# k's halves swapped by GpSimd, the crossbar from the second batch on, and regrouped remainder work in a fused attention and MLP kernel

## The chip, the cores and the metric

The kernel runs on one core of one Trainium2 chip. The metric is the device time of one execution in microseconds (us); less is better. A core has TensorE (PE; its weight loads are PEld), VectorE (DVE), ScalarE (ACT), GpSimd (POOL) and SyncE (SP), which here only issues DMAs. "Crossbar" means the transpose done by a DMA (DMA_TRANSPOSE).

## The reference

Thresholded attention over 8 batches of 8 heads with 576 positions and head size 64, then a two-layer MLP over the 4608 tokens (512 to 2048 to 512).

```python
scores = scale * np.matmul(q, k.transpose(0, 1, 3, 2))
thresh = np.max(scores, axis=-1, keepdims=True) - tau
scores = np.where(scores >= thresh, scores, -1000000000.0)
scores = scores - np.max(scores, axis=-1, keepdims=True)
attn = np.exp(scores)
attn = attn / (np.sum(attn, axis=-1, keepdims=True) + 1e-09)
return np.matmul(attn, v).astype(np.float32)
...
x = np.ascontiguousarray(attn_out.transpose(0, 2, 1, 3)).reshape(B * S, H * D)
...
h = x @ w_in
g = h - np.tanh(h)
return (g @ w_out).astype(np.float32)
```

## The kernel before

Two heads make a pair; there are 32 pairs, four per batch. A head's 576 positions are 512 in four blocks of 128 and a remainder of 64. A pair has nine score tiles of 128 query rows by 576 keys: tiles 0 to 3 are the first head's blocks, tile 4 (kind "M") the remainders of both heads, 64 rows each, tiles 5 to 8 the second head's blocks. Of these, "A" and "B" tiles follow each other in twos.

q and k are split into a high and a low fp16 part (khl, qhl; from the second pair on GpSimd does it, L160 to L164), turned on TensorE (ps_k, ps_q, L186) and copied to SBUF by VectorE (kT, qT, L192). The scores are q times kT plus q times kS, where kS is kT with its two halves of 64 partitions swapped. Pair 0 gets kS from TensorE (L198), all others by two DMAs from SyncE (L208, L209).

The main loop runs one step per tile, and its order is written out by hand. Step s issues: nb of tile s+6 (L257), the scores of tile s+7 on TensorE (psS, L232 and L242) with VectorE's copy and row maximum (sc, L248), the masking activation of tile s+5 on ScalarE (z, L274), the exponentials of tile s (pT, L302 or L310), a share of the MLP (psH L391, tanh th L404, g L410, psY L417, yo L426), and the product with v of tile s-2 (psO, L341, for M tiles L329). Between z and pT the masked scores are turned. Tiles below NPE (72, the first two batches) are turned on TensorE into psZ (L293), the others through the crossbar (zT, L282). After a head's tiles follows the division by the row sums (rc, osb, L355 and L356), and after a pair emit_x turns its result for the MLP (psX, L367; the remainder L374; copies L381 and L382).

A table (PREP) says how many steps ahead of a pair's first scores its loads (16 to 14 steps), splits (8, 7), turns (5, 3) and the cast of v (4) are issued. The weights are loaded in 16 pieces and cast by GpSimd (L473), one piece every four steps up to step 56. Each batch's MLP layers run spread over the next batches' tiles; a last "batch" of all remainders (xR, 512 tokens) and what is left runs behind the loop. Its output goes out by one store per 128 tokens, from yo, which has two buffers (L433); scratch for scores (ps_big) has two buffers too.

Of the kernel before, what the change touches and what calls it, by code (L numbers as in the profile page):

```python
# [18 lines left out]
def kernel(  # L19
# [11 lines left out]
    nc = tc.nc  # L31
    P = 128

    B, H, S, D = q.shape
# [6 lines left out]
    QKSC = 256.0  # L41
# [4 lines left out]
    HPAIR = H // 2  # L46
# [3 lines left out]
    TPP = 9  # L50
    NTILE = NPAIR * TPP


    NPE = 2 * HPAIR * TPP
    W = 2 * S

    AHEAD = 7
# [6 lines left out]
    MB = 512  # L64
# [52 lines left out]
    ps_y = pool("ps_y", 1, space=PSUM)  # L117

    ctx.enter_context(tc.manual_schedule())
    warm = const.tile([P, 1], F32, name="warm")  # L120
    nc.vector.memset(warm, 0.0)
    nc.scalar.activation(out=warm, in_=warm, func=ACT.Exp)


    raws = {}
# [3 lines left out]
    def load(p, t):  # L129
        b, h0 = p // HPAIR, 2 * (p % HPAIR)  # L130
        hs = slice(h0, h0 + 2)
        src = {"k": k, "q": q, "v": v}[t]
        eng = nc.scalar if p == 0 and t == "q" else nc.sync
        r = raws[p, t] = raw_pool.tile([P, 10, D], F32, name=f"{t}raw", tag=t)
        n = 8 if t == "v" else 10
        eng.dma_start(
            out=r[:, 0:n, :].rearrange("p (h c) d -> p h (c d)", h=2)[:, :, 0 : 4 * D],
            in_=src[b, hs, 0:512, :].rearrange("h (p c) d -> p h (c d)", c=4),
        )
        if t == "v":  # L140
            rem = src[b, hs, 512:S, :].rearrange("h s d -> s h d")
# [7 lines left out]
    def split(p, t, fast=False):  # L149
        r = raws.pop((p, t))[:, 0:9, :]  # L150
        hl = hl_pool.tile([P, TPP, 2, D], FP16, name=f"{t}hl", tag=t)
        if fast:
            nc.scalar.mul(out=hl[:, :, 0, :], in_=r, mul=QKSC)
            nc.vector.scalar_tensor_tensor(
                out=hl[:, :, 1, :], in0=r, scalar=QKSC, in1=hl[:, :, 0, :],
                op0=ALU.mult, op1=ALU.subtract,
            )
        else:
            x = hl_pool.tile([P, TPP, D], F32, name="xs", tag="xs")
            nc.gpsimd.tensor_scalar(  # L160
                out=x, in0=r, scalar1=QKSC, scalar2=1.0, op0=ALU.mult, op1=ALU.mult
            )
            nc.gpsimd.tensor_copy(out=hl[:, :, 0, :], in_=x)
            nc.gpsimd.tensor_tensor(  # L164
                out=hl[:, :, 1, :], in0=x, in1=hl[:, :, 0, :], op=ALU.subtract
            )
        hls[p, t] = hl

    def split_v(p):
        r, vb = raws.pop((p, "v")), vbs[p % NV]  # L170
# [8 lines left out]

    mats = {}  # L180

    def turn(p, t):
        hl = hls.pop((p, t))
        ps = ps_big.tile([P, W], FP16, name=f"ps_{t}", tag="big")
        for c in range(TPP):
            nc.tensor.matmul(  # L186
                out=ps[:, c * P : (c + 1) * P],
                lhsT=hl[:, c, :, :].rearrange("p a d -> p (a d)"),
                rhs=ident_f16, is_transpose=True, start=True, stop=True,
            )  # L190
        m = qk_pool.tile([P, W], FP16, name=f"{t}T", tag=t)
        nc.vector.tensor_copy(out=m, in_=ps)  # L192
        mats[p, t] = m
        if t == "k" and p == 0:
            ps = ps_big.tile([P, W], FP16, name="ps_ks", tag="big")
            for c in range(TPP):
                for a in range(2):
                    nc.tensor.matmul(  # L198
                        out=ps[64 * a : 64 * a + 64, c * P : (c + 1) * P],
                        lhsT=hl[:, c, 1 - a, :],  # L200
                        rhs=ident_f16, is_transpose=True, start=True, stop=True,
                    )
            sw = qk_pool.tile([P, W], FP16, name="kS", tag="ks")
            nc.vector.tensor_copy(out=sw, in_=ps)
            mats[p, "ks"] = sw
        elif t == "k":
            sw = qk_pool.tile([P, W], FP16, name="kS", tag="ks")
            nc.sync.dma_start(out=sw[0:D, :], in_=m[D:P, :])  # L208
            nc.sync.dma_start(out=sw[D:P, :], in_=m[0:D, :])  # L209
            mats[p, "ks"] = sw  # L210


    MAIN = (slice(0, 512), slice(640, W))
# [101 lines left out]
    def attend(i):  # L315

        p, j = divmod(i, TPP)
        kd, vb = kind(j), vbs[p % NV]
        if kd == "A":
            return  # L320
        if j in (1, 6):
            ops[p, int(j > 4)] = ps_o.tile([P, 5, D + 1], F32, name="psO", tag="o")
        po = ops[p, int(j > 4)]
        if kd == "M":
            pt = pts.pop(i)
            for c in range(5):
                n = 64 if c == 4 else P
                for hh in range(2):
                    nc.tensor.matmul(  # L329
                        out=po[64 * hh : 64 * hh + 64, 4, :],  # L330
                        lhsT=pt[0:n, c * P + 64 * hh : c * P + 64 * hh + 64],
                        rhs=vb[0:n, hh, c, :], start=(c == 0), stop=(c == 4),
                    )
            return
        pt, hh = pts.pop(i), int(j > 4)

        for ab in range(2):
            blocks = [(4 * ab + ab + c, c) for c in range(4)]
            blocks.append((4, 4 + ab))
            for n, (blk, c) in enumerate(blocks):  # L340
                nc.tensor.matmul(  # L341
                    out=po[:, (j - 1 - 5 * hh) + ab, :],
                    lhsT=pt[:, blk * P : (blk + 1) * P], rhs=vb[:, hh, c, :],
                    start=(n == 0), stop=(n == 4),
                )
# [3 lines left out]
    def norm(p, hh):  # L349
        po = ops.pop((p, hh))  # L350
        if hh == 0:
            osb[p] = o_pool.tile([P, 5, 2, D], BF16, name="osb")
        n = 5 - hh
        rc = st_pool.tile([P, 5], F32, name="rc", tag="rc")
        nc.vector.reciprocal(out=rc[:, 0:n], in_=po[:, 0:n, D])  # L355
        nc.vector.tensor_tensor(  # L356
            out=osb[p][:, 0:n, hh, :], in0=po[:, 0:n, 0:D],
            in1=rc[:, 0:n].unsqueeze(2).to_broadcast([P, n, D]), op=ALU.mult,
        )

    xs = {}

    def emit_x(p):
        o = osb.pop(p)
        ps = ps_h.tile([P, S], BF16, name="psX", tag="h")
        for t in range(4):
            nc.tensor.matmul(  # L367
                out=ps[:, t * P : (t + 1) * P],
                lhsT=o[:, t, :, :].rearrange("p a d -> p (a d)"),
                rhs=ident_bf, is_transpose=True, start=True, stop=True,  # L370
            )
        for hh in range(2):
            s = slice(64 * hh, 64 * hh + 64)
            nc.tensor.matmul(  # L374
                out=ps[s, 512:576], lhsT=o[s, 4, 0, :], rhs=ident_bf[s, s],
                is_transpose=True, start=True, stop=True,
            )
# [4 lines left out]
        nc.vector.tensor_copy(out=xR[:, p % HPAIR, b, :], in_=ps[:, 512:S])  # L382


    gs, stores = {}, []
# [29 lines left out]
    def project(m, ms, part, ps, last):  # L415
# [5 lines left out]
        if part == 3:  # L421
            yo = y_pool.tile([P, d_model], F32, name="yo")
            if last:
                nc.scalar.copy(out=yo, in_=ps)
            else:
                nc.vector.tensor_copy(out=yo, in_=ps)  # L426
            if m < B:
                rows = out[m * S : m * S + MB, :].rearrange("(p c) n -> c p n", c=4)
                to = rows[ms]
# [3 lines left out]
            stores.append(lambda: nc.sync.dma_start(out=to, in_=yo))  # L433

    def layers(m, tail):

# [69 lines left out]
    for t in ("k", "q", "v"):  # L506
        load(0, t)
    for t in ("k", "q"):
        split(0, t, fast=True)
    for t in ("k", "q"):  # L510
        turn(0, t)
    split_v(0)
    for t in ("k", "q", "v"):
        load(1, t)
# [8 lines left out]
    for s in range(-AHEAD, NTILE + LAG + 3):  # L523
# [7 lines left out]
            shift(s + AHEAD - 1)  # L531
        if 0 <= s + AHEAD < NTILE:
            scores(s + AHEAD)
        if 0 <= s + MASK < NTILE:
            kink(s + MASK)
        bend()
# [79 lines left out]
```

## Time and profile before

| What | us |
|---|---|
| median of 3 runs (range) | 579.23 (577.52 to 580.37) |
| the profiled execution, its own time | 578.05 |
| its span | 576.3 |
| PE busy | 535.3 |
| DVE busy | 442.6 |
| ACT busy | 440.1 |
| POOL busy | 215.6 |

The span is what the profiler saw of the program; its time is a little longer. Busy time says how long an engine had work in flight, not whether the run waited for it; that is read from the chain of work that ended last, which goes back from the last instruction, at each step to what released it.

### The profile page before, as it was taken

What the parts mean: (1) busy time and instruction counts of PE and PEld (TensorE: products, weight loads), DVE (VectorE), ACT (ScalarE), POOL (GpSimd) and SP (SyncE); (2) the same over time, 40 slices, a digit from 0 to 9 for tenths busy, and PEclk for the clock granted to TensorE, in tenths of its full rate; (3) what the DMA queues carried; (4) which work ended last, traced back from release to release, by engine and by line L of the source; (5) the groups of instructions that cost most, each with busy time, mean ns of one, the idle gap of its engine ahead of it and who ended that gap; (6) DMA issues with size and microseconds to landing.
All of it is one profiled execution on the core that took longest, in us unless ns stands there. A gap on an engine that the chain in (4) does not pass through costs nothing.

```text
span 576.3 us, 13882 instructions
## 1 busy us (share of the span) xinstructions
PE 535.3 (93%) x5146; PEld 303.6 (53%) x5146; DVE 442.6 (77%) x1312; ACT 440.1 (76%) x634; POOL 215.6 (37%) x310
## 2 busy tenths in 40 slices
PE   3889899999999999998999999999999999999990
PEld 2566566665555555554555555555555555444440
DVE  3888888888988988888888888888889896444410
ACT  1889898898888898887898988888889888333400
POOL 6646683753433344444444343345333400000000
PEclk9999999999999999999999999999999999999996
DMA  6556755448889999779989999998999865110111
GB/s 180 170 170 175 211 171 160 138 109 176 176 180 183 180 197 197 173 179 185 174 192 182 186 196 178 188 203 189 179 185 176 184 128 120 38 38 36 38 45 46
DMA packets 186923, 89.48 MB, mean 155 GB/s; under 512 B 150632, under 2 KB 175208, under 8 KB 186856
## 3 DMA queue, kind: packets, MB, share of 16 engines
q1 hardware_dynamic: 186454, 88.31, 70.2%
q8 instruction: 40, 0.66, 0.5%
q10 hardware_dynamic: 402, 0.29, 0.2%
q14 instruction: 27, 0.22, 0.1%
HBM read 37.75 MB, written 9.44 MB: 82 GB/s over the span
## 4 chain that ended last, share of the span: by engine, by line
PE 75%; DMA 6%; ACT 6%; DVE 6%; POOL 2%; issue 1%; SPq 1%; ACTq 0%; POOLq 0%; DVEq 0%
PE psY L417 20%; PE psH L391 17%; PE psS L242 17%; PE psO L341 5%; PE ps_k L186 3%; PE psS L232 3%; ACT pT L302 3%; DVE sc L248 3%; DMA kS<-kT 2%; PE psHt L391 2%; PE psZ L293 2%; ACT z L274 2%; PE psO L329 2%; PE ps_q L186 2%; DMA out_dram<-yo 2%
## 5 line engine op out<-in xcount | busy, mean ns | idle before, releaser
L248 DVE TENSOR_SCALAR_CACHE_REDUCE sc<-psS 128x576 f32<-128x576 f32 x288 | 216.4, 751 | 24.4 <-PE psS L232 10.8
L274 ACT ACTIVATE z<-sc,nb 128x576 bf16<-128x576 f32 x256 | 195.5, 768 | 27.2 <-DVE nb L257 26.0
L417 PE MATMUL psY<-w_out_sb,g 128*128 128x512 bf16 x576 | 145.4, 379 | 0.0
L310 ACT ACTIVATE pT<-zT 128x1152 f16<-128x1152 bf16 (+1 forms) x120 | 127.9, 1066 | 11.6 <-DMA zT<-z 11.0
L391 PE MATMUL psH<-xT,w_in_sb 128*128 128x512 bf16 x480 | 123.4, 379 | 0.0
L242 PE MATMUL psS<-kT,qT 128*128 128x512 f16 (+1 forms) x512 | 105.7, 288 | 8.4 <-DVE nb L257 4.7
L242 PEld LDWEIGHTS <-qT 128*128 128x128 f16 x1024 | 74.8, 98 | 70.7 <-issue 12.4
L242 PE MATMUL psS<-kS,qT 128*128 128x512 f16 (+1 forms) x512 | 105.8, 289 | 2.7 <-DMA kS<-kT 2.6
L410 DVE SCALAR_TENSOR_TENSOR g<-th,psH 128x512 bf16<-128x512 f32 x128 | 87.3, 682 | 25.3 <-ACT th L404 25.1
L404 ACT ACTIVATE th<-psH 128x512 f32<-128x512 f32 x128 | 74.5, 582 | 18.6 <-PE psH L391 18.4
L160 POOL TENSOR_SCALAR xs<-kraw 128x576 f32<-128x576 f32 x31 | 20.8, 669 | 165.9 <-DMA kraw<-in_k_dram 120.3
L417 PEld LDWEIGHTS <-g 128*128 128x128 bf16 x576 | 49.6, 98 | 57.7 <-issue 2.5
L391 PEld LDWEIGHTS <-w_in_sb 128*128 128x128 bf16 x576 | 48.9, 98 | 54.2 <-issue 2.7
L341 PEld LDWEIGHTS <-pT 128*128 128x128 f16 x1280 | 55.6, 98 | 24.3 <-ACT pT L310 2.1
L341 PE MATMUL psO<-vb,pT 128*128 128x65 bf16 x1280 | 61.2, 193 | 0.6 <-ACT pT L310 0.6
L302 ACT ACTIVATE pT<-psZ 128x640 f16<-128x640 bf16 (+1 forms) x72 | 47.1, 654 | 10.6 <-PE psZ L293 10.5
L257 DVE TENSOR_SCALAR nb<-mx 128x1 f32<-128x1 f32 x288 | 42.5, 147 | 3.4
L164 POOL TENSOR_TENSOR qhl<-xs,qhl 128x576 f16<-128x576 f32 x31 | 39.7, 1279 | 2.6
L164 POOL TENSOR_TENSOR khl<-xs,khl 128x576 f16<-128x576 f32 x31 | 39.6, 1279 | 2.7
L274 ACT ACTIVATE zm<-sc,nb 128x576 bf16<-128x576 f32 x32 | 24.7, 773 | 17.3 <-DVE nb L257 17.1
L192 DVE COPY qT<-ps_q 128x1152 f16<-128x1152 f16 x32 | 24.2, 755 | 11.5 <-PE ps_q L186 11.5
L426 DVE COPY yo<-psY 128x512 f32<-128x512 f32 x30 | 20.7, 689 | 13.7 <-DMA out_dram<-yo 8.0
(60 smaller groups left out, 505.5 us busy)
## 6 DMA issues: line engine op xcount, KB each, us to landing
out_dram<-yo SPq DMA_DIRECT2D x36, 256.0 KB
kS<-kT SPq DMA_DIRECT2D x62, 144.0 KB
kraw<-in_k_dram SPq DMA_DIRECT2D x32, 256.0 KB
vraw<-in_v_dram SPq DMA_DIRECT2D x32, 256.0 KB
qraw<-in_q_dram SPq DMA_DIRECT2D x31, 256.0 KB
wt<-in_moe_w_in_dram SPq DMA_DIRECT2D x8, 512.0 KB
wt<-in_moe_w_out_dram SPq DMA_DIRECT2D x8, 512.0 KB
vraw<-in_v_dram SPq DMA_DIRECT2D x64, 32.0 KB
```

The source lines that it names most:

```text
L164: nc.gpsimd.tensor_tensor(out=hl[:, :, 1, :], in0=x, in1=hl[:, :, 0, :], op=ALU.subtract)
L242: nc.tensor.matmul(out=ps[:, dst], lhsT=lhs, rhs=kk[:, src], start=(n == 0), stop=(n == 1),)
L248: nc.vector.tensor_scalar(out=sc, in0=ps[:, lo : lo + S], scalar1=SC, scalar2=None, op0=ALU.mult, op1=ALU.max, accum_out=mx,)
L257: nc.vector.tensor_scalar(out=nb, in0=mx, scalar1=-1.0, scalar2=tau, op0=ALU.mult, op1=ALU.add)
L274: nc.scalar.activation(out=z, in_=sc, func=ACT.Prelu, bias=nb, scale=1.0, alpha=STEEP)
L302: nc.scalar.activation(out=pt[:, off * P : (off + n) * P], in_=ps[:, 0 : n * P], func=ACT.Exp)
L310: nc.scalar.activation(out=pt[:, 0 : n * P], in_=zts.pop(i)[:, 0:n, :], func=ACT.Exp)
L341: nc.tensor.matmul(out=po[:, (j - 1 - 5 * hh) + ab, :], lhsT=pt[:, blk * P : (blk + 1) * P], rhs=vb[:, hh, c, :], start=(n == 0), stop=(n ...
L391: nc.tensor.matmul(out=ps, lhsT=w_in_sb[:, c, n * P : (n + 1) * P], rhs=xs[m][:, c, :] if m < B else xR[:, c, :, :], start=(c == 0), stop= ...
L404: nc.scalar.activation(out=th, in_=ps, func=ACT.Tanh)
L410: nc.vector.scalar_tensor_tensor(out=gs[m][:, n, :], in0=th, scalar=-1.0, in1=ps, op0=ALU.mult, op1=ALU.add,)
L417: nc.tensor.matmul(out=ps, lhsT=gs[m][:, n, ms * P : (ms + 1) * P], rhs=w_out_sb[:, n, :], start=(n == 0), stop=(n == DF_C - 1),)
```

## The change

- **Turning the masked scores.** NPE falls from 72 to 36: batch 1 (pairs 4 to 7) goes through the crossbar too.
- **Swap of k.** For pairs 1 to 31 GpSimd copies the two halves of kT into kS; the two DMAs go.
- **Remainder of k and q.** It is loaded as "s h d" (positions outside, heads inside) instead of "h s d"; the turn of that chunk reads the identity in a strided order, so that kT and qT are as before.
- **M tiles.** Five matmuls take both heads' v at once (130 columns, all 128 rows) in place of ten 64-wide ones. The half that belongs to the other head is set to zero in the division, by a new VectorE instruction with the mask own. emit_x folds the two halves with one matmul (fold) in place of two 64x64 turns.
- **First pair.** Its loads, splits and turns are issued in two parts: the first head's four chunks and the remainder first, the rest at the second and third step of the loop. ScalarE takes some of the copies. All of the first pair's scratch comes from other buffers than ps_big.
- **Last stores.** The remainder's output goes out as two stores of 64 rows per 128 tokens instead of one with an outer dimension of 2.

```diff
-    NPE = 2 * HPAIR * TPP
+    NPE = HPAIR * TPP
...
+    own = const.tile([P, 2, D], BF16, name="own")
+    nc.vector.memset(own, 0.0)
+    nc.vector.memset(own[0:64, 0, :], 1.0)
+    nc.vector.memset(own[64:P, 1, :], 1.0)
+    fold = const.tile([P, 64], BF16, name="fold")
+    nc.vector.tensor_tensor(
+        out=fold, in0=ident_bf[:, 0:64], in1=ident_bf[:, 64:P], op=ALU.add
+    )
...
+        rem = src[b, hs, 512:S, :].rearrange("h s d -> s h d")
...
-            eng.dma_start(out=r[:, 4, :], in_=src[b, hs, 512:S, :])
+            eng.dma_start(out=r[:, 4, :], in_=rem)
+
+    def load_first(t, eng):
...
+        for h in range(2):
+            eng.dma_start(
+                out=r[:, 5 * h : 5 * h + 4, :].rearrange("p c d -> p (c d)"),
+                in_=src[0, h, 0:512, :].rearrange("(p c) d -> p (c d)", c=4),
+            )
+            if h == 0:
+                rem = src[0, 0:2, 512:S, :].rearrange("h s d -> s h d")
+                eng.dma_start(out=r[:, 4, :], in_=rem)
+
+    load_first("k", nc.sync)
+    load_first("q", nc.scalar)
...
+    def split_first(t, part):
+        cs = (slice(0, 5), slice(5, TPP))[part]
...
+    by_head = lambda ap: ap.rearrange("p (s h) -> p h s", h=2)
+    in_heads = lambda ap: ap.rearrange("p (h s) -> p h s", h=2)
+
+    def turn_chunk(out, c, lhsT):
+        rhs = ident_f16
+        if c == 4:
+            out, rhs = in_heads(out), by_head(rhs)
+        nc.tensor.matmul(
+            out=out, lhsT=lhsT, rhs=rhs, is_transpose=True, start=True, stop=True
+        )
...
-        elif t == "k":
-            sw = qk_pool.tile([P, W], FP16, name="kS", tag="ks")
-            nc.sync.dma_start(out=sw[0:D, :], in_=m[D:P, :])
-            nc.sync.dma_start(out=sw[D:P, :], in_=m[0:D, :])
-            mats[p, "ks"] = sw
+        if t == "k":
+            sw = qk_pool.tile([P, W], FP16, name="kS", tag="ks")
+            nc.gpsimd.tensor_copy(out=sw[0:D, :], in_=m[D:P, :])
+            nc.gpsimd.tensor_copy(out=sw[D:P, :], in_=m[0:D, :])
+            mats[p, "ks"] = sw
+
+    def turn_first(t, part):
...
+        if part == 1 or t == "q":
+            nc.scalar.copy(out=dst, in_=ps[:, 0:n])
+        else:
+            nc.vector.tensor_copy(out=dst, in_=ps[:, 0:n])
...
             for c in range(5):
-                n = 64 if c == 4 else P
-                for hh in range(2):
-                    nc.tensor.matmul(
-                        out=po[64 * hh : 64 * hh + 64, 4, :],
-                        lhsT=pt[0:n, c * P + 64 * hh : c * P + 64 * hh + 64],
-                        rhs=vb[0:n, hh, c, :], start=(c == 0), stop=(c == 4),
-                    )
+                nc.tensor.matmul(
+                    out=po[:, 4:6, :], lhsT=pt[:, c * P : (c + 1) * P],
+                    rhs=vb[:, :, c, :], start=(c == 0), stop=(c == 4),
+                )
...
+        if hh == 0:
+            nc.vector.scalar_tensor_tensor(
+                out=osb[p][:, 4, :, :], in0=po[:, 4:6, 0:D], scalar=rc[:, 4:5],
+                in1=own, op0=ALU.mult, op1=ALU.mult,
+            )
...
-        for hh in range(2):
-            s = slice(64 * hh, 64 * hh + 64)
-            nc.tensor.matmul(
-                out=ps[s, 512:576], lhsT=o[s, 4, 0, :], rhs=ident_bf[s, s],
-                is_transpose=True, start=True, stop=True,
-            )
+
+        nc.tensor.matmul(
+            out=pf[:, 256:320], lhsT=o[:, 4, :, :].rearrange("p a d -> p (a d)"),
+            rhs=fold, start=True, stop=True,
+        )
...
-                rows = out.rearrange("(b s) n -> b s n", b=B)
-                to = rows[2 * ms : 2 * ms + 2, MB:S, :]
-            stores.append(lambda: nc.sync.dma_start(out=to, in_=yo))
+                for h in range(2):
+                    b = 2 * ms + h
+                    stores.append(
+                        lambda b=b, h=h: nc.sync.dma_start(
+                            out=out[b * S + MB : (b + 1) * S, :],
+                            in_=yo[64 * h : 64 * h + 64, :],
+                        )
+                    )
...
+        if s == 1 - AHEAD:
+            for t in ("k", "q"):
+                split_first(t, 1)
+        if s == 2 - AHEAD:
+            for t in ("k", "q", "ks"):
+                turn_first(t, 1)
```

Three places in the programs of the engines. First TensorE in a full batch, at the end of emit_x (osb is the pair's result, qT the next score tile's queries). Before:

```order
L367 LDWEIGHTS osb
L367 MATMUL psX<-ident_bf,osb 128x128
L374 LDWEIGHTS osb
L374 MATMUL psX<-ident_bf,osb 64x64
L374 LDWEIGHTS osb
L374 MATMUL psX<-ident_bf,osb 64x64
L242 LDWEIGHTS qT
L242 MATMUL psS<-kT,qT 128x512
```

After:

```order
L421 LDWEIGHTS osb
L421 MATMUL psX<-ident_bf,osb 128x128
L427 LDWEIGHTS osb
L427 MATMUL psX<-fold,osb 128x64
L292 LDWEIGHTS qT
L292 MATMUL psS<-kT,qT 128x512
```

Two matmuls on a quarter of the array have become one on all of it; the masked tile's attend, one L378 row "psO<-vb,pT 128x130" five times instead of ten 64x65 rows, has changed in the same way.

Second GpSimd, early in batch 0, from the split of pair 2's q on (xs and qhl belong to the split, wt is a piece of the weights, vb is v of pair 2). Before:

```order
L160 TENSOR_SCALAR xs<-qraw 128x576
L163 CAST qhl<-xs 128x9x64
L164 TENSOR_TENSOR qhl<-xs,qhl 128x9x64
L473 CAST w_in_sb<-wt 128x1024
L171 CAST vb_81<-vraw 128x2x4x64
```

After:

```order
L179 TENSOR_SCALAR xs<-qraw 128x576
L182 CAST qhl<-xs 128x9x64
L183 TENSOR_TENSOR qhl<-xs,qhl 128x9x64
L531 CAST w_in_sb<-wt 128x1024
L237 COPY kS<-kT 64x1152
L238 COPY kS<-kT 64x1152
L202 CAST vb_81<-vraw 128x2x4x64
```

The two copies stand between the weight cast and the cast of v, and wait for kT; on SyncE the two DMAs of L208 and L209 at this step are gone.

Third SyncE, the end of its program (yo is the output tile). Before:

```order
L282 DMA_TRANSPOSE zT<-z 128x9x128 x2
L433 DMA out_dram<-yo 128x512 x10
L433 DMA out_dram<-yo 2x64x512 x4
L611 UNCONDITIONAL_BRANCH
```

After:

```order
L332 DMA_TRANSPOSE zT<-z 128x9x128 x2
L482 DMA out_dram<-yo 128x512 x10
L487 DMA out_dram<-yo 64x512 x8
L674 UNCONDITIONAL_BRANCH
```

Four stores with an outer dimension of two have become eight of 64 rows.

More of the change, by code (lines that the diff above doesn't have):

```diff
@@ L132, in load @@
         src = {"k": k, "q": q, "v": v}[t]
-        eng = nc.scalar if p == 0 and t == "q" else nc.sync
+        eng = nc.sync
         r = raws[p, t] = raw_pool.tile([P, 10, D], F32, name=f"{t}raw", tag=t)
@@ L185, in turn @@
         for c in range(TPP):
[L186 to L189, printed above, removed]
+            turn_chunk(
+                ps[:, c * P : (c + 1) * P], c, hl[:, c, :, :].rearrange("p a d -> p (a d)")
             )
@@ L321, in attend @@
         if j in (1, 6):
-            ops[p, int(j > 4)] = ps_o.tile([P, 5, D + 1], F32, name="psO", tag="o")
+            ops[p, int(j > 4)] = ps_o.tile([P, 6, D + 1], F32, name="psO", tag="o")
         po = ops[p, int(j > 4)]
@@ L364, in emit_x @@
         o = osb.pop(p)
-        ps = ps_h.tile([P, S], BF16, name="psX", tag="h")
+        pf = ps_h.tile([P, 320], F32, name="psX", tag="h")
+        ps = pf[:, 0:256].bitcast(BF16)
         for t in range(4):
@@ L504 @@
             plan.setdefault(first - d, []).append(lambda p=p, f=f: f(p))
-    for t in ("k", "q", "v"):
-        load(0, t)
+    load(0, "v")
     for t in ("k", "q"):
-        split(0, t, fast=True)
-    for t in ("k", "q"):
-        turn(0, t)
+        split_first(t, 0)
+    for t in ("k", "q", "ks"):
+        turn_first(t, 0)
     split_v(0)
```

77 lines of the change are left out of this document (41 added, 36 removed).

## The prediction, made before the changed kernel was run

> **What bounds the kernel now.** I read the chain of work that ended last first, then busy time by stage, then the rows of the engines that the change loads. In the middle of the run the chain is TensorE back to back. This is one head pair of nine tiles in batch 2 (start, length, work):
>
> ```profile
> 154.35 0.40 PE psO L329 x10
> 154.74 0.61 PE ps_k L186 x9
> 155.35 0.49 PE psS L242 x4
> ...
> 158.37 0.50 PE ps_q L186 x9
> ...
> 164.60 0.32 PE psO L341 x10
> 164.91 0.22 PE psX L367 x4
> 165.14 0.15 PE psX L374 x2
> 165.28 0.60 PE psS L242 x4
> ...
> 170.39 0.61 PE ps_k L186 x9
> ```
>
> From ps_k to the next ps_k is 15.65 us, with no other engine in it: in this stage a TensorE microsecond saved is a microsecond of the run, until VectorE or ScalarE is next. Two places stand out. The same four score matmuls (psS) take 0.60 behind the 64x64 matmuls of L374, and 0.49 elsewhere. The same nine transposes take 0.61 behind the 64-wide matmuls of L329 (ps_k), and 0.50 behind full ones (ps_q). So each group of partial matmuls costs the next work 0.11 us more.
>
> The stages, cut where the swap of k of pairs 1, 5, 9/10 and 14 is issued (columns: window, length, busy of PE, PEld, DVE, ACT, POOL with instructions, clock, DMA share, GB/s):
>
> ```profile
> 18.80:68.80 50.00, 43.85 (x590) 30.62 (x589) 41.73 (x138) 44.19 (x70) 29.18 (x39) 1.00 0.66 194
> 68.80:126.80 58.00, 55.99 (x680) 36.93 (x680) 49.39 (x157) 52.72 (x88) 38.03 (x51) 1.00 0.50 144
> 141.10:202.50 61.40, 60.52 (x591) 33.85 (x590) 53.95 (x163) 52.87 (x73) 25.02 (x36) 1.00 0.92 180
> 555.40:576.30 20.90, 6.22 (x29) 2.65 (x27) 0.69 (x1) 0.58 (x1) 0.00 (x0) 0.76 0.12 47
> ```
>
> The four pairs of batch 0 take 50.0 us with ScalarE at 88% and PE, DVE close below. Batch 1 takes 58.0: all three at 85 to 97%. Batches 2 to 7 take about 61 each, PE at 99%, DVE at 88%, DMA at 92%. In the last 21 us nearly nothing runs, and the DMA share is 0.12, about 2 engines of 16.
>
> **The end: -10 us.** The remainder's output leaves by four stores. The chain, the last copy (ScalarE), and SyncE's issue and last wait:
>
> ```profile
> 546.95 7.79 PE psY L417 x36
> ...
> 555.41 9.59 DMA out_dram<-yo
> ...
> 565.09 0.58 ACT yo L424
> ```
> ```profile
> L433 SPq DMA_DIRECT2D out_dram<-yo x36: 332/570/651, 163.6 to 565.7; - x36
> ```
> ```profile
> SPq L611 <- DMA out_dram<-yo: 8.9, 1, 8.9
> ```
>
> One store takes 9.59 us, and yo has two buffers, so the third and fourth copies wait for stores. Left alone, PE finishes the 36 matmuls at 554.73 and the last 32 of them, at 7.79/36 = 0.216 us, at 561.65. Then comes one copy (0.58), two issues instead of one (2 x 0.57) and the landing. A store on all engines: at eight times the engines 9.59 becomes 1.2; the quiet upper row is a 512 KB weight load, 4.55 us (58.85, quoted below). I take 2.9, the middle. 561.65 + 0.6 + 1.1 + 2.9 = 566.3 against 576.3: **-10**, bounds -8.3 to -11.7.
>
> The Trainium skill, "DMA: Bandwidth & Descriptors", section on why a DMA increments its semaphore by 16, says that the number of engines is the largest up to 16 that divides the slowest dimension of both access patterns. By that rule the old store, with its outer dimension of 2, had two engines, which agrees with the share of 0.12, and the new ones, with 64 rows, have 16. The same page's rules for kernel authors say of two transfers to disjoint partition halves not to bother, because they share the same engines; by that rule alone the split would bring nothing, which is the fourth rival. The trace speaks for the first rule.
>
> **TensorE in batches 2 to 7: -7 us.** The masked-tile attend goes from ten 64-wide matmuls (0.40) to five of 130 columns. The nearest rows are 128 columns at 0.22/4 = 0.056 and 65 columns at 0.032, so five take 0.28: -0.12, and -0.11 on the transposes behind. emit_x goes from two 64x64 matmuls (0.15) to one with 64 columns (0.03 to 0.06): -0.10, and -0.11 on the scores behind. Together 0.44 per pair, 24 pairs: -10.6. Against it: two turned chunks per pair read the identity with a stride, which no row shows; between nothing and twice the 0.056, up to +2.7 in all. And DVE gets one more instruction per pair:
>
> ```profile
> L356 DVE TENSOR_TENSOR osb<-psO,rc 128x320 bf16<-128x320 f32 x32 | 15.7, 491 | 1.1
> L356 DVE TENSOR_TENSOR osb<-psO,rc 128x256 bf16<-128x256 f32 x32 | 13.6, 424 | 1.1
> ```
>
> The slope is 1.05 ns per element over some 155, so 128 elements take 290, less 67 on the shortened one: +0.22. DVE's 53.95 per batch becomes 54.8 of 59.6, 92%. It is near to being the bound, so I take two thirds: **-7**, between -10.6 and -2.
>
> **The swap of k: -2 us.** Before, two DMAs per pair, issued on SyncE behind the wait for kT:
>
> ```profile
> PEld L242 <- DMA kS<-kT: 4.2, 5, 2.2
> ```
> ```profile
> SPq L208 <- DVE nb L257: 64.9, 27, 9.3
> ```
>
> PE waited for them in few pairs, 4 us in all, and SyncE stood 64.9 us there with transposes and loads queued behind. Both go. The remainder loads of k and q also change from an outer dimension of 2 to 64. The xR copy reads f32 instead of bf16, still 64 columns: nothing. I take **-2**, bounds 0 and -5. GpSimd gets two copies of 64x1152 per pair; its rows:
>
> ```profile
> L473 POOL CAST w_in_sb<-wt 128x1024 bf16<-128x1024 f32 x8 | 8.3, 1037 | 20.5 <-DMA wt<-in_moe_w_in_dram 16.5 <-PE psX L374 4.0
> L171 POOL CAST vb<-vraw 128x512 bf16<-128x512 f32 x32 | 19.9, 623 | 8.3 <-DMA vraw<-in_v_dram 4.9 <-PE psS L242 1.9 <-PE psO L341 1.4
> L164 POOL TENSOR_TENSOR qhl<-xs,qhl 128x576 f16<-128x576 f32 x31 | 39.7, 1279 | 2.6
> ```
>
> One-input slope 0.81 ns per element: 1.14 us per copy; at the two-input rate (2.2 ns) 2.56. They stand behind the split of q and ahead of split_v. The first scores that read kS come five steps after the turn, five ninths of 12.5 to 15.3 us, so 7 to 8.5 us; 2.3 us fit. But GpSimd is not idle in batch 0, where the chain already runs through it (columns as in the first fence):
>
> ```profile
> 50.25 1.04 POOL w_in_sb L473
> 51.29 0.65 POOL xs L160
> ...
> 52.74 1.29 POOL khl L164
> ...
> 54.08 0.68 PE ps_k L186 x9
> ...
> 58.85 4.55 DMA wt<-in_moe_w_in_dram
> ```
>
> The split of k waits behind a weight cast, that one for a load. GpSimd has 29.18/4 = 7.3 of 12.5 us per pair there; 9.6 after. What queues behind a copy that waits for kT is split_v, a cast and the next split of k. I add **+0.5**, range 0 to +4.
>
> **Batch 1 by the crossbar: -1 us.** PE loses 164 transposes (328 rows of psZ to 164 in PE's program). ScalarE per pair, from:
>
> ```profile
> L310 ACT ACTIVATE pT<-zT 128x1152 f16<-128x1152 bf16 x96 | 110.6, 1152 | 11.6 <-DMA zT<-z 11.0 <-PE psS L242 0.5
> L310 ACT ACTIVATE pT<-zT 128x640 f16<-128x640 bf16 x24 | 17.4, 723 | 0.0
> L302 ACT ACTIVATE pT<-psZ 128x640 f16<-128x640 bf16 x40 | 28.0, 701 | 2.6 <-PE psZ L293 2.6
> L302 ACT ACTIVATE pT<-psZ 128x512 f16<-128x512 bf16 x32 | 19.1, 596 | 8.1 <-PE psZ L293 7.9
> ```
>
> 5 x 0.701 + 4 x 0.596 = 5.89 becomes 4 x 1.152 + 0.723 = 5.33, so 52.7 falls to 50.5 per batch; DVE goes to 50.3. At the 88% that ScalarE and DVE reach in the neighbouring stages that is 57.3: -1. What PE saves is off the path. The 20 transposes need DMA: batch 2 has 0.92 x 61.4 = 56.5 us of it, batch 1 0.50 x 58 = 29. The difference, 27.5, is the transposes with four stores, less the weight loads that only batch 1 has. Batch 1 would carry 56 to 64 of 58 us. **-1**, from -4 to +6.
>
> **The start: -4 us.**
>
> ```profile
> 5.83 0.68 ACT L153 ACTIVATE khl<-kraw 128x576 f16<-128x576 f32 x1 [3.60 <-DMA kraw<-in_k_dram]
> ...
> 7.36 1.14 PE L186 MATMUL ps_k<-ident_f,khl 128*128 128x128 f16 x9 [7.36 <-DVE khl L154]
> ...
> 9.55 0.76 DVE L192 COPY kT<-ps_k 128x1152 f16<-128x1152 f16 x1
> ...
> 11.52 0.76 DVE L192 COPY qT<-ps_q 128x1152 f16<-128x1152 f16 x1 [0.55 <-PE ps_q L186]
> ...
> 13.51 0.76 DVE L248 TENSOR_SCALAR_CACHE_REDUCE sc<-psS 128x576 f32<-128x576 f32 x1 [1.24 <-PE psS L242]
> ```
>
> The first scores wait for whole loads, five DVE pieces of about 0.76 and three turns. After, five of nine chunks go first, and q's copy is ScalarE's: four pieces of 0.42 for 3.8, -2.1; turns -1.0; the half load about -1.5; the second halves of the splits come back on DVE, +0.7. The constants own and fold cost nothing while DVE and ScalarE wait for the first load (3.60 above); without that cover it would be some 0.4, four rows of DVE. **-4**, bounds +0.4 (loads no earlier, more issues) and -5.
>
> **Sum.** -10 - 7 - 2 + 0.5 - 1 - 4 = -23.5. The profiled execution took 578.05 (span 576.3 and 1.75 around it), 1.2 below the median of 579.23. 578.05 - 23.5 = **554.5**.
>
> **Rivals.**
> 1. DMA is the bound in batch 1: 64 us of it exposed, +6 instead of -1, so 561.5. For: the weight loads share the queue with the first transposes. Against: loads run 16 steps ahead, and the swap's DMAs are gone. 0.14.
> 2. VectorE takes over in batches 2 to 7: instead of -7 only -1, so 560.5. For: 92%. Against: PE had no wait in the pair above at 88%. 0.13.
> 3. GpSimd is late, and the kernel is **slower**. With t per copy, batch 0 loses 4 x (7.3 + 2t - 12.5) and three pairs of batch 1 3 x (38.03/4 + 2t - 14.5); that eats 23.5 us from t = 4.2. At 4.6, where batches 2 to 7 (25.02/4 + 9.2 against 15.2) lose too, it is about 590. For: a copy across partitions stands in no row. Against: it is four times the one-input rate. 0.03.
> 4. The end stays, halves no faster than the whole: 564.5. Against: the share of 0.12. 0.04.
>
> The forecast keeps 0.65, and 0.02 is left for several of these at once that end within 0.5% of before (what a measurement of this kernel can tell from no change). Range 545 to 564: it takes in rivals 1 and 2 and most of the single bounds. Forecast and rivals 1, 2 and 4 make faster by over 0.5% 0.95; within it 0.02; slower 0.03.
>
> **What would show it.** Right: the last store lands under 5 us after its issue and the span ends near 564; ps_k behind the masked attend at 0.50, psS behind emit_x at 0.49, a pair at 15.2; the first sc near 9.5; batch 1 at 57 with DMA near 1.0; no PE wait for kS; GpSimd's copies near 1.14. Wrong: waits of ScalarE for zT in batch 1, of PE for khl or kS in batch 0, or a pair that DVE sets.

## The result, and the profile after

| | before | after |
|---|---|---|
| median (range), 4 runs each | 578.87 us (577.52 to 580.37) | 554.71 us (553.51 to 555.38) |
| the profiled execution, its own time | 578.05 | 554.70 |
| its span | 576.3 | 552.9 |

The ratio is 0.958, 95% interval 0.955 to 0.9609: 24 us faster. The forecast of 554.5 met the total, but several of its terms missed and the misses cancelled; the experiments below show which.

To compare stages between kernels I cut every trace at the same event, the start of VectorE's copy of kT of a pair (kT1 is that of pair 1). From the copy of pair 1 to that of pair 5 is called batch 0 here, from 5 to 9 batch 1, from 9 to 31 the middle, and from 31 to the end of the span the rest. The copies start at 18.04, 68.06, 126.02 and 461.07 us before and at 15.75, 63.97, 124.53 and 448.95 us after:

| us | start | batch 0 | batch 1 | middle | rest | span |
|---|---|---|---|---|---|---|
| before | 18.0 | 50.0 | 58.0 | 335.1 | 115.2 | 576.3 |
| after | 15.8 | 48.2 | 60.6 | 324.4 | 103.9 | 552.9 |
| difference | -2.3 | -1.8 | +2.6 | -10.7 | -11.3 | -23.4 |

Four stages became shorter and one longer: batch 1. Single readings of the start scatter: over the ten kernels of this document that load the first pair's remainder as the change does, the copy of pair 1 starts between 14.9 and 17.0 us, over the four that load it as before between 17.5 and 19.0. The same stages in the windows view of after (window, length, busy of PE, PEld, DVE, ACT, POOL with instructions, clock, DMA share, GB/s); the lines answer to the four of before:

```profile
15.80:64.00 48.20, 42.53 (x569) 30.52 (x569) 42.20 (x143) 45.29 (x72) 42.49 (x53) 1.00 0.55 165
64.00:124.50 60.50, 48.42 (x501) 28.55 (x499) 50.10 (x159) 51.53 (x72) 42.45 (x52) 0.97 1.02 214
137.90:197.00 59.10, 58.18 (x562) 33.40 (x561) 53.25 (x165) 52.45 (x72) 34.47 (x44) 1.00 0.78 168
538.00:552.90 14.90, 10.36 (x49) 4.51 (x46) 1.38 (x2) 1.17 (x2) 0.00 (x0) 0.97 0.30 70
```

In batch 1 PE falls from 56 to 48 us, and the stage is longer all the same: the DMA share went from 0.50 to 1.02. In the third line PE is still at 98%, and DMA fell from 0.92 to 0.78, since the swap's DMAs are gone. In the last line the quiet tail is gone.

The chain in batch 2 of after (start, length, work), at the two places where the matmuls changed:

```profile
151.96 0.29 PE psO L378 x5
152.25 0.50 PE ps_k L221 x9
...
159.02 0.69 DVE yo L479
...
167.38 0.29 PE psO L378 x5
167.67 0.50 PE ps_k L221 x9
...
177.74 0.22 PE psX L421 x4
177.97 0.03 PE psX L427
178.00 0.49 PE psS L292 x4
```

The attend of the masked tile takes 0.29 (0.40 before) and the transposes behind it 0.50 (0.61); the fold takes 0.03 (0.15) and the scores behind it 0.49 (0.60). From ps_k to ps_k are 15.42 us against 15.65. A piece of VectorE (yo) now stands in the chain of a full batch.

The end of the chain, SyncE's last wait, and the stores' DMA row (KB each, median us from issue to landing):

```profile
539.95 8.43 PE psY L470 x39
...
548.45 0.59 ACT yo L477
```
```profile
SPq L674 <- DMA out_dram<-yo: 1.7, 2, 1.1
```
```profile
out_dram<-yo SPq DMA_DIRECT2D x8, 128.0 KB, 2.3
```

PE runs through to the last copy, no store of 9.59 us stands between, and a store lands in 2.3 us.

### The profile page after: what moved, and what is told of

Read it like the earlier page. It is cut to its first block, busy times and chain, and to the rows that moved or that the text cites. A ratio compares the mean times of both kernels' runs of the same rounds, so it can differ in the third digit from the quotient of the medians.

```text
span 552.9 us, 13222 instructions
## 1 busy us (share of the span) xinstructions
PE 515.4 (93%) x4790; PEld 294.0 (53%) x4790; DVE 444.7 (80%) x1349; ACT 442.5 (80%) x624; POOL 286.6 (52%) x372
## 4 chain that ended last, share of the span: by engine, by line
PE 68%; DVE 15%; ACT 8%; DMA 5%; issue 2%; POOL 1%; SPq 0%; ACTq 0%; DVEq 0%; POOLq 0%
PE psY L470 20%; PE psH L444 17%; PE psS L292 15%; DVE sc L298 6%; PE psO L389 5%; ACT z L324 3%; PE psS L282 3%; DMA zT<-z 3%; PE psHt L444 2%; DVE g L463 2%; PE ps_q L221 2%; ACT pT L352 2%; PE ps_k L221 2%; ACT pT L360 2%; DVE yo L479 1%
## 5 line engine op out<-in xcount | busy, mean ns | idle before, releaser
L360 ACT ACTIVATE pT<-zT 128x1152 f16<-128x1152 bf16 (+1 forms) x140 | 149.2, 1065 | 6.1 <-DMA zT<-z 2.5
L444 PE MATMUL psH<-xT,w_in_sb 128*128 128x512 bf16 x480 | 124.7, 381 | 2.0 <-DVE g L463 1.7
L292 PEld LDWEIGHTS <-qT 128*128 128x128 f16 x1024 | 76.1, 98 | 73.7 <-issue 20.4
L237 POOL COPY kS<-kT 64x1152 f16<-64x1152 f16 x31 | 35.3, 1140 | 133.6 <-DVE nb L307 133.4
L292 PE MATMUL psS<-kS,qT 128*128 128x512 f16 x496 | 101.7, 287 | 0.0
L324 ACT ACTIVATE zm<-sc,nb 128x576 bf16<-128x576 f32 x32 | 24.8, 774 | 23.3 <-DVE nb L307 23.3
L238 POOL COPY kS<-kT 64x1152 f16<-64x1152 f16 x31 | 35.4, 1142 | 1.3
L221 PE MATMUL ps_k<-ident_f,khl 128*128 128x128 f16 x288 | 22.4, 224 | 8.9 <-DVE khl L195 6.7
```

The lines of the kernel that those rows point to most:

```text
L221: nc.tensor.matmul(out=out, lhsT=lhsT, rhs=rhs, is_transpose=True, start=True, stop=True)
L292: nc.tensor.matmul(out=ps[:, dst], lhsT=lhs, rhs=kk[:, src], start=(n == 0), stop=(n == 1),)
L324: nc.scalar.activation(out=z, in_=sc, func=ACT.Prelu, bias=nb, scale=1.0, alpha=STEEP)
L360: nc.scalar.activation(out=pt[:, 0 : n * P], in_=zts.pop(i)[:, 0:n, :], func=ACT.Exp)
L444: nc.tensor.matmul(out=ps, lhsT=w_in_sb[:, c, n * P : (n + 1) * P], rhs=xs[m][:, c, :] if m < B else xR[:, c, :, :], start=(c == 0), stop= ...
```

## The experiments

Differences are of medians in us. An interval of a ratio is 0.0015 to 0.0036 wide to each side, and beside the runs, which were on several chips, the kernel before had medians from 578.22 to 579.67. So differences below about 2 us between kernels are not told apart by the times alone. Where I say "in the profile", it is the stages of one profiled execution.

**The last stores.** The change, but the two stores per 128 tokens are cut by columns, so that each keeps the outer dimension of 2.

```diff
-                            out=out[b * S + MB : (b + 1) * S, :],
-                            in_=yo[64 * h : 64 * h + 64, :],
+                    cs = slice(256 * h, 256 * h + 256)
+                            out=rows[2 * ms : 2 * ms + 2, MB:S, cs], in_=yo[:, cs]
```

> The changed kernel, but each of the last four outputs is cut by columns: two stores of 2 x 64 rows x 256 columns, whose outer dimension is 2, in place of two stores of 64 rows x 512. The bytes and the number of stores are the same. If the outer dimension sets how many engines work, the end is as long as before the change: 564 to 566, the DMA share there near 0.12. If it is enough that there are two smaller stores, it stays at 554 to 556.

Measured: 562.85, ratio 0.9722 (0.9701 to 0.9743), 8.1 above the change and a little under the 564 to 566 expected; in the profile the rest is 114.9 instead of 103.9. In its chain half the bytes take nearly as long as the whole store before (9.59):

```profile
542.74 9.36 DMA out_dram<-yo
```

That isn't the time of one such store alone: several are in flight at once, and from 548.9 to the end the DMA share is 0.12 at 44 GB/s, against 0.12 at 47 GB/s in the last 20.9 us before. Eight stores with the old outer dimension are as slow together as four, so it is the outer dimension that confined the store, not the number of DMAs. The end is worth 8.1 by medians and 11.0 in the profiles; this profiled execution took 565.74, 2.9 more than its median.

**The masked tile's attend and the fold, alone.** The kernel before with only the five wide matmuls, own and fold.

```diff
+                nc.tensor.matmul(
+                    out=po[:, 4:6, :], lhsT=pt[:, c * P : (c + 1) * P],
+                    rhs=vb[:, :, c, :], start=(c == 0), stop=(c == 4),
+                )
```

> The kernel before with only the masked tiles' attend in five matmuls, the mask own in the division and the fold in emit_x. Theory (TensorE sets batches 2 to 7, so its 0.45 us per pair come through but for what VectorE's added 342 ns instruction takes): kT of pair 9 to kT of pair 31 falls from 335.1 by 6 to 9 us, the run to 570 to 573. Rival (VectorE takes over): 1 to 2 us, the run at 577 to 578.

Measured: 572.09, ratio 0.9905 (0.9877 to 0.9934), -6.1 against the kernel before beside it (578.22); the middle is 328.1 in the profile, -7.0. The times run from 569.76 to 574.35, and the profiled execution is the fastest of them.

**The crossbar in batch 1.** The change with NPE back at 72, and the kernel before with only NPE at 36.

```diff
-    NPE = HPAIR * TPP
+    NPE = 2 * HPAIR * TPP
```

> The changed kernel with NPE = 72 again: batch 1 back on TensorE, all else as changed. In the changed kernel batch 1 (kT of pair 5 to kT of pair 9) took 60.6 us, 2.6 more than before, with a DMA share of 1.02. Theory A (the crossbar's DMAs collide there with the loads of the weights): batch 1 falls below the 58.0 of before, to about 56 to 57, since the attend savings on TensorE stay; the run takes 550 to 551. Rival B (the loss is GpSimd's queue, where the copies of kS and the weight casts hold up the next split of k): batch 1 stays at 59 to 61 and the run at 554 to 555.

> The kernel before with NPE = 36 as its only change. Theory A: batch 1 gets longer by 3 to 6 us because the crossbar, the swap's DMAs and the weight loads share the queue; the run takes 581 to 585. Rival B: with no copies on GpSimd the crossbar does in batch 1 what the prediction's term said, -1 us, so 577 to 579.

Measured: the change with 72 takes 552.32, ratio 0.9539 (0.9518 to 0.956), 2.4 less than the change; batch 1 is 57.4 in the profile. The kernel before with 36 takes 584.01, ratio 1.0091 (1.006 to 1.0122): 4.6 slower than the kernel before beside it (579.46), with batch 1 at 65.1 instead of 58.0 in its longest execution. This part of the change is a loss, and with the swap's DMAs still there a larger one. The chain of batch 1 in after says through what:

```profile
71.94 6.28 DMA zT<-z
...
86.47 4.74 DMA zT<-z
...
93.13 4.77 DMA zT<-z
...
99.55 5.02 DMA wt<-in_moe_w_out_dram
104.58 0.05 issue
104.63 1.04 POOL w_out_sb L531
105.67 0.65 POOL xs L179
...
108.45 1.14 PE ps_k L221 x9
109.59 0.96 PE psS L292 x4
110.55 1.51 PE psH L444 x4
```

ScalarE waits for transposes, and GpSimd's split of k stands behind a weight cast that waits for its load. When the split has come, TensorE also works more slowly for a while: between 108.4 and 112.0 us its granted clock is 0.54, and the nine transposes of ps_k take 1.14 us where they take 0.50 in batch 2. Over the stage the clock is 0.97. Its matmuls keep PE busy for 48.4 us, and the same ones for 46.6 us at clock 1.00 in the kernel that follows here, so by estimate 1.8 us of batch 1 are this slower clock. What lowers it no run here shows.

To see whether it is the collision of the two kinds of DMA, one kernel leaves out seven of eight loads of w_out:

```diff
+        if cols >= width and i > 0:
+            loaded.append((flat, kept[0], i, cols))
+            return
```

> The changed kernel, but of the eight pieces of w_out only the first is loaded, and it is cast eight times (the other seven eighths of w_out are left out). GpSimd's and TensorE's work and the 20 transposes in batch 1 stay as they are; 3.5 MB of loads in batch 1 go. Theory A (crossbar and weight loads collide): batch 1 falls from 60.6 to 57 to 58 and the run to 551 to 552. Rival B (GpSimd's order alone) or C (the transposes alone are too much for the queue): batch 1 stays at 60 to 61.

Measured: 546.68, ratio 0.9454 (0.9439 to 0.947), batch 1 at 53.0, a larger gain than theory A expected. That is 4.4 less than with TensorE's transposes (57.4), but the kernel with those still loads all of w_out; TensorE's transposes without the loads were not run. Batch 1 of the two:

```profile
65.00:122.40 57.40, 54.32 (x659) 36.48 (x657) 50.15 (x160) 52.98 (x88) 42.51 (x52) 1.00 0.39 117
```
```profile
63.80:116.80 53.00, 46.65 (x503) 28.09 (x501) 49.60 (x159) 50.80 (x72) 42.53 (x53) 1.00 0.89 174
```

The first is NPE at 72, the second the one load of w_out. The DMA share at which batch 1 took 60.6 was 1.02. Taking away either the transposes or the loads shortens the stage, so the loss comes from the two together. GpSimd's wait for w_out (11.4 us in after) and ScalarE's for transposes (2.5, and 1.5 for those of M tiles) are both gone with one load; which of them costs how much was not separated.

**w_out loaded earlier: a better kernel.** w_out is read for the first time in batch 2, and in batch 0 the DMA share is 0.55. Nothing is left out here.

```diff
+    wo_pool = pool("wo", 6)
...
+    early, pieces, kept = pieces[8:14], iter(pieces[:8] + pieces[14:]), []
...
+            if early and s + AHEAD >= 13 and (s + AHEAD) % 4 == 1:
+                w_load(early.pop(0), wo_pool, kept)
+            if s + AHEAD == 35:
+                loaded[:0] = kept
```

> The change, but six of the eight w_out pieces are loaded during batch 0 (one every four steps, into six buffers of their own) and wait there; GpSimd casts them at the same steps as in the change. Nothing is left out. Theory A, the loads of w_out collide with the first transposes of batch 1: with them moved, batch 1 falls from 60.6 us to about 54 to 55 (53.0 with seven of eight loads left out) and the run to about 549; batch 0, DMA share 0.55 over 48.2 us, has room for 6 x 4.7 us and stays within 1 us. Theory B, batch 0 cannot take them, because its chain runs through weight loads and GpSimd too: batch 0 grows by 3 us or more and the run stays at 553 to 556.

Measured: 549.42 (548.42 to 550.31), ratio 0.9481 (0.945 to 0.9513), 5.3 below the change. Batch 0 stays at 48.2, batch 1 is 55.0:

```profile
15.70:64.20 48.50, 42.55 (x572) 30.36 (x569) 42.36 (x141) 44.94 (x72) 41.47 (x52) 1.00 0.72 227
64.20:118.50 54.30, 45.59 (x490) 27.55 (x496) 48.96 (x157) 50.29 (x71) 43.47 (x53) 1.00 0.84 178
```

The DMA share is 0.72 and 0.84 in place of 0.55 and 1.02: the same loads, placed where there was room.

**The swap of k.** The change, with kS filled by SyncE's two DMAs again.

```diff
-            nc.gpsimd.tensor_copy(out=sw[0:D, :], in_=m[D:P, :])
-            nc.gpsimd.tensor_copy(out=sw[D:P, :], in_=m[0:D, :])
+            nc.sync.dma_start(out=sw[0:D, :], in_=m[D:P, :])
+            nc.sync.dma_start(out=sw[D:P, :], in_=m[0:D, :])
```

> The changed kernel with the two copies of kS by DMA from SyncE as before, all else as changed. Theory A: batch 1 has still more DMA and gets longer, 62 or more, and some 0.1 to 0.5 us per pair return in batches 2 to 7; the run takes 557 to 562. Rival B: batch 1 falls to 58 or less, since GpSimd's queue is free, and the run takes 551 to 553. If the swap on GpSimd is worth the 2 us that the prediction gave it outside batch 1, that much comes back in batches 2 to 7.

Measured: 564.03, ratio 0.9742 (0.9722 to 0.9762), 9.3 above the change and above the 557 to 562 of theory A; in the profile 3.4 more in batch 0, 2.6 in batch 1 and 3.9 in the middle, and 0.8 less at the start. This is the largest gap between the prediction and a measurement. Three causes were possible: the wait that holds SyncE's queue, the bytes, and the landing that TensorE waits for. Two more kernels add them one by one to the change, while GpSimd goes on filling the kS that TensorE reads. First two tiny DMAs from kT in the old place, into a tile kd that nothing reads, then the whole halves into it:

```diff
+            nc.sync.dma_start(out=kd[0:1, 0:64], in_=m[D:D + 1, 0:64])
+            nc.sync.dma_start(out=kd[D:D + 1, 0:64], in_=m[0:1, 0:64])
```
```diff
+            nc.sync.dma_start(out=kd[0:D, :], in_=m[D:P, :])
+            nc.sync.dma_start(out=kd[D:P, :], in_=m[0:D, :])
```

> The change, GpSimd swaps k, and SyncE in addition issues per pair, where the swap's two DMAs stood, two DMAs of 64 elements each from kT into a tile that nothing reads. So SyncE waits for kT as before and moves next to no bytes. Theory A, the swap's 9.3 us are mostly SyncE's queue, held by the wait while loads and transposes stand behind it: the run is at 560 to 563, batch 0 near 51 us and SyncE's wait on that line 15 us or more between 14.9 and 66.5 us. Theory B, they are the transfers themselves (bytes on the DMA engines, TensorE waiting for kS to land): the run is at 555 to 556.

> As e12_hold_only, but the two DMAs carry both whole halves (64x1152 each), into a tile that nothing reads; TensorE reads GpSimd's kS and waits for no DMA of it. Against e12_hold_only it adds the bytes, and the run with the swap by DMA (e2_swap_dma, 564.0) adds to it TensorE's waits for kS, less GpSimd's copies. Theory A: within 1 us of e12_hold_only and 562 to 564, so neither bytes nor landing matter. Theory B1, the bytes matter: 2 us or more above e12_hold_only, mostly in batches 1 and later, where the DMA share is highest. Theory B2, the landing matters: it stays 2 us or more below 564.

Measured: 564.07 (ratio 0.9747, 0.9731 to 0.9763) with the tiny ones, 563.16 (0.9735, 0.9713 to 0.9757) with the whole halves. By the totals two DMAs with next to no bytes bring back all of the loss, and neither the bytes nor the landing add to it. The split is not quite clean. The kernel with the swap by DMA has no copies on GpSimd, and it loses more in batch 1 (2.6 against 0.9) and less in the middle (3.9 against 6.1) than the one with the tiny DMAs, so equal totals hide unequal parts. And the tiny DMAs also take SyncE's time to issue (0.58 and 0.59 us), which no run separates from the wait. Where the hold costs, in batch 0 of the kernel with the tiny DMAs, from its chain:

```profile
44.55 1.05 POOL w_in_sb L534
45.60 0.02 issue
45.62 0.35 SPq L546
45.97 0.05 issue
46.02 4.67 DMA kraw<-in_k_dram
50.69 1.27 POOL khl L183
...
58.63 5.31 DMA kraw<-in_k_dram
...
63.99 1.29 POOL khl L183
65.28 0.05 issue
65.32 0.68 PE ps_k L221 x9
```

At the end of this stretch TensorE's transposes wait for the split of k. The two rows of kraw must not be read as waits of that split: the load issued at 46.02 takes 6.5 us to land, so it lands behind the khl that the chain puts after it, and GpSimd's own timeline shows the split (xs, then khl) running without a gap. What GpSimd waited for is in the wait list of batch 0 (14.9 to 66.5 us; us in total, times, longest):

```profile
SPq L240 <- DVE nb L310: 16.9, 4, 5.2
...
PE ps_k L221 <- POOL khl L183: 2.8, 2, 1.4
...
POOL w_in_sb L534 <- DMA wt<-in_moe_w_in_dram: 5.9, 3, 2.6
```

SyncE stands 16.9 us for kT, a piece of the weights that the change issues at 38.24 us is issued at 44.60, GpSimd's cast waits for such pieces (5.9 us, none in the change), and the split of k stands behind the cast. With the swap itself by DMA that wait of GpSimd is 19.9 us in batch 0.

In the middle (124 to 449 us) it is the transposes that are issued late; the change has no such row there:

```profile
ACT pT L363 <- DMA zT<-z: 13.4, 17, 2.0
```

**The start.** The change, with the first pair whole as before (but its remainder loaded "s h d"), and then the same with that remainder as before.

```diff
-    for t in ("k", "q"):
-        split_first(t, 0)
+    for t in ("k", "q", "v"):
+        load(0, t)
+    for t in ("k", "q"):
+        split(0, t, fast=True)
```
```diff
+            two = src[b, hs, 512:S, :]
+            eng.dma_start(out=r[:, 4, :], in_=two if p == 0 else rem)
```

> The changed kernel with pair 0 loaded, split and turned whole, as before. If the first pair in two parts is worth what kT of pair 1 shows (15.8 against 18.0 us), that comes back and stays: 556.5 to 557.5. If the prediction's 4 us are right and only the second parts hide them at that place: 558 to 559. If batch 0 is set by loads and not by its start: 554.7 to 555.5.

> As the run with the first pair whole (e10_first_whole), but the remainder of k and q of the first pair is loaded with the outer dimension of 2, as before. Theory A, the start's 2.3 us come from that load, which had two engines: VectorE's copy of kT of pair 1 comes at 18.0 us as in the kernel before, and the run is about 557. Theory B, they come from elsewhere (GpSimd's copies for pair 1, other buffers): the copy comes at 15.7 us and the run is 555.

Measured: 554.85 (0.9591, 0.9568 to 0.9614) and 556.06 (0.9603, 0.9567 to 0.9639). The times hardly tell them apart; the traces do. VectorE's first row maximum and its copy of kT of pair 1, in after, with the first pair whole, and with the old remainder load too:

```profile
9.74 0.76 DVE L298 TENSOR_SCALAR_CACHE_REDUCE sc<-psS 128x576 f32<-128x576 f32 x1 [0.73 <-PE psS L292]
...
11.86 0.88 DVE L195 SCALAR_TENSOR_TENSOR qhl<-qraw,qhl 128x256 f16<-128x256 f32 x1
...
15.75 0.75 DVE L233 COPY kT<-ps_k 128x1152 f16<-128x1152 f16 x1
```
```profile
11.56 0.76 DVE L314 TENSOR_SCALAR_CACHE_REDUCE sc<-psS 128x576 f32<-128x576 f32 x1 [0.76 <-PE psS L308]
...
15.73 0.75 DVE L239 COPY kT<-ps_k 128x1152 f16<-128x1152 f16 x1
```
```profile
13.72 0.76 DVE L317 TENSOR_SCALAR_CACHE_REDUCE sc<-psS 128x576 f32<-128x576 f32 x1 [1.24 <-PE psS L311]
...
18.15 0.75 DVE L241 COPY kT<-ps_k 128x1152 f16<-128x1152 f16 x1
```

In two parts the first scores come 1.8 us earlier, and the second parts, on the same VectorE, give all of it back by pair 1. The old remainder load costs 2.4 us there, as much as the two groups of kernels under the first table differ. Batch 1 was 1.6 us shorter in that profile (58.4 against 60.0), which leaves 0.8 at pair 9; but its granted clock was 1.00 against 0.97, with PE busy for 46.4 us against 48.4, so the shorter stage need not come from the load. How much of the 2.4 reaches the run stays open: the medians differ by 1.2.

**The remainder loads of pairs 1 to 31.** The change, with those loads and the identity as before.

```diff
+            eng.dma_start(out=r[:, 4, :], in_=src[b, hs, 512:S, :])
...
+                heads=True,
```

> The changed kernel with the remainder of k and q loaded as before, outer dimension 2, for pairs 1 to 31, and turned with the plain identity. If the two engines that such a load has hold up the queue, batches 0 and 1 get longer, where GpSimd waits for loads, by 1 to 3 us each, and the run takes 556 to 560. If not, it stays at 554 to 555; and if the strided identity costs TensorE anything, batches 2 to 7 get shorter by some tenths per batch.

Measured: 555.65, ratio 0.9616 (0.9597 to 0.9635), 0.9 above the change: not told apart from nothing, and between the two forecasts. In the profile batch 0 is the same (48.2) and batch 1 is 62.0 against 60.6, at a granted clock of 0.94 against 0.97. A full batch takes 59.1 to 59.2 with the plain and with the strided identity, so the stride costs nothing that shows.

## Why the prediction was right or wrong, point by point

| Term | predicted | measured, and by what |
|---|---|---|
| the end | -10 | -8.1 (stores by columns) |
| TensorE in batches 2 to 7 | -7 | -6.1 (alone, on the kernel before) |
| swap of k, with GpSimd's cost | -1.5 | -9.3 (swap by DMA) |
| remainder of pairs 1 to 31 | in the swap's term | -0.9 (not told apart from 0) |
| batch 1 by the crossbar | -1 | +2.4 (NPE at 72) |
| start | -4 | -0.1 for the two parts, -1.2 for the remainder load (neither told apart from 0) |
| sum | -23.5 | -23.3 |

Each measured term is one part undone or done alone. That they add up to nearly the difference of -24.2 does not show that the parts are independent: the crossbar in batch 1 costs 2.4 in the change, beside GpSimd's swap, and 4.6 in the kernel before, beside the swap's DMAs. The total was right by luck, because errors cancelled: the swap and the remainder were 8.7 too small, and against them stood batch 1 with 3.4, the start with 2.7, the end with 1.9 and TensorE with 0.9. Of the signs that the prediction named, one of being wrong appeared, ScalarE's waits for zT in batch 1, and a piece of VectorE stood in a pair's chain. Its "the span ends near 564" did not fit its own sum: that is the end alone, with none of the other terms.

- **The end** was right in its mechanism; its size, 8.1 by medians, is just under the lower bound of 8.3, and 11.0 in the profiles is within. Rival 4 fell: the same bytes in two DMAs stay slow when the outer dimension is 2 (9.36), and each store takes 2.3 with 64 rows. The Trainium skill, "DMA: Bandwidth & Descriptors", section "Why a DMA increments its semaphore by 16 and not by 1", has the number of engines as the largest up to 16 that divides the slowest dimension of both access patterns; both times agree with that.
- **TensorE** was right: attend 0.29 for 0.28, fold 0.03, and the 0.11 behind each group of partial matmuls gone. VectorE's added instruction takes 342 ns for an estimated 290. Of the 0.44 us per pair, 0.32 were left in the run with this part alone (7.0 over 22 pairs), and VectorE's pieces in the chain are a little of rival 2: the two thirds taken for that were about right, though a pair takes 15.42 us and not the 15.2 named as a sign.
- **The swap** is the step that failed most. The prediction quoted the 64.9 us that SyncE stood at L208, said that transposes and loads queue behind it, and then took its price from PE's direct wait for kS (4.2), with a bound of 5. The price lay with what stands behind: late weight loads, then GpSimd, then PE's wait for khl in batch 0 (2.4 us with the tiny DMAs, in the profile); late transposes, then ScalarE, in the middle (6.1). Holding the queue with two tiny DMAs per pair was shown to cost 9.4. That is with the rest of the change in place; on the kernel before, with fewer transposes in the queue, the swap alone was not run. GpSimd's copies took the estimated 1.14 us and no wait of PE for kS is left, so rival 3 had no ground; the group of one of them in after:

```profile
L237 POOL COPY kS<-kT 64x1152 f16<-64x1152 f16 x31 | 35.3, 1140 | 133.6 <-DVE nb L307 133.4
```

GpSimd now stands in the wait for kT (133.4 us in all), as SyncE did with 64.9; in the chain of batch 2 no GpSimd work appears.
- **Batch 1.** "Batch 1 would carry 56 to 64 of 58 us" of DMA was right (1.02 of 60.5), and the step to -1 was wrong: it let ScalarE's and VectorE's usual 88% set the stage. Rival 1 had the mechanism, with +6 as its price; it cost 2.4. What it came from is shown by the loads of w_out left out (-7.6 in batch 1) and moved (-5.6). In neither of those is TensorE's clock below 1.00 in that stage, so some 2 us of each difference are, by estimate, the slower clock behind the waits, which the prediction didn't have.
- **The start.** The first row maximum came at 9.74, as forecast, and that sign proved nothing: the second halves of the splits "come back on DVE, +0.7" was too little, they took back all of it. The gain at pair 1 is that of the remainder load, which the prediction had put into another term and priced at nothing here; in the run's time it is not told apart from nothing.

Still open: why one execution of the stores by columns took 2.9 us more than its median, what lowers TensorE's clock in batch 1, and how much of the batch-0 gain would go to each load that SyncE holds up.

## What to carry to other kernels

A wait on an in-order DMA queue is priced by what stands behind it, not only by who waits for the transfer itself: follow the queued loads and transposes to their readers. Before work is moved to the DMA engines, add up their share stage by stage; where it passes 1.0, move loads that aren't needed yet to a stage with room. A first result that comes earlier is worth only what is still earlier at the next steady point, so measure there. A transfer's row in a chain is a wait of the next row only if it lands before that begins, so compare it with the wait list and the engine's timeline.

## What was not expected of the hardware

- Two DMAs of 64 elements per pair, whose data nothing reads, cost 9.4 us in a run (554.71 to 564.07), as much as two of 144 KB within what the times can tell (8.5).
- A transpose takes longer to land beside weight loads. The transposes' DMA row (median us to landing) of the change between 64 and 118 us, and between 130 and 400 us:

```profile
zT<-z SPq DMA_TRANSPOSE x14, 4.7
```
```profile
zT<-z SPq DMA_TRANSPOSE x74, 3.4
```

With six of the eight w_out pieces moved, those between 64 and 118 us land in 3.3, so it is the loads and not the stage:

```profile
zT<-z SPq DMA_TRANSPOSE x17, 3.3
```

- Behind a wait in batch 1 TensorE's granted clock averaged 0.54 for 3.6 us (108.4 to 112.0 us of the change), and nine transposes took 1.14 us instead of 0.50. With the old remainder load of the first pair TensorE waits there too (1.7 us for khl), and the clock stays at 1.00.

- The first pair's remainder of q with an outer dimension of 2 also takes longer to issue on ScalarE's queue than with 64 rows, 1.13 us against 0.64 (old and new load, first pair whole):

```profile
1.74 1.13 ACTq L153 DMA_DIRECT2D qraw<-in_q_dram  x1
```
```profile
1.74 0.64 ACTq L152 DMA_DIRECT2D qraw<-in_q_dram  x1
```
